# One batch laid out apart from the others: nine consecutive tokens per partition, five loads, softmax in three parts, and a different order of the first weight conversions

## The chip, the cores and the metric

The kernel runs on one core of one Trainium2 chip. The metric is the device time of one execution in microseconds (us); lower is better.

## The reference, cut to what matters

Three stages follow one another, all in float32: an attention over a small memory, a layer with a "tanh-shrink", and a max-out layer. The weights come as float64 (eight bytes each).

```python
# q, k, v: (8, 8, 576, 64) = batch, head, token, dim;  phi: (8, 8, 576, 32)
a = exp(phi - max over tokens);  a = a / (sum over tokens + 1e-9)
k_m, v_m = a^T k, a^T v                       # per batch and head: 32 x 64
attn = softmax(q k_m^T / 8);  x = attn v_m    # per token: 32 weights
x = x as (4608, 512)
h = x w_in;  g = h - tanh(h);  x = g w_out    # w_in 512 x 2048, w_out 2048 x 512
out = max(x w1, x w2, x w3) @ w_out2          # w1..w3 512 x 768, w_out2 768 x 512
```

## The kernel before, in words

**Products.** A float32 product that must be exact enough is done as three matmuls of halves: each operand is split into a rounded high part and a remainder (`mm3`: high by high, high by low, low by high). So every operand of the two big layers goes through a cast on ScalarE (ACT) and a subtraction on VectorE (DVE) or GpSimd (POOL) first. Float64 weights are turned into float32 by `conv` (lines 160 to 180): two ACT operations, three DVE operations, and one POOL operation (W_in) or two POOL operations and one more on ACT (W_out).

**Attention of a batch.** `kv_gen` (line 295) is `phi_gen` and then `kv_mm`: the maximum of phi over the tokens on DVE, transposed on TensorE (PE) and reduced, spread again by a matmul, subtracted, exponentiated on ACT; then k_m, v_m and the sums as PE products into one PSUM bank, normalised (`rc`, `n`), transposed (`ps_t`) into `kT` and `vT`. `q_gen` (line 302) does the softmax in two halves of 288 tokens: the queries are transposed on DVE in 32 x 32 blocks (`qT`), multiplied with `kT` (`sc`), transposed back (`s`), then maximum, subtraction, exponential, sum, reciprocal (`st`), product on POOL, transposition (`aT`), and the split into `at` (cast on ACT, remainder on POOL). v_m is folded into W_in: `vw_gen` (line 353) makes vw = v_m W_in (`ps_w`) for a batch and a quarter `fq` of W_in's 2048 columns, so that h = at vw.

**The two big layers.** A step is one tile of tokens by one block `fc` of 128 hidden columns: `emit_h` 6 matmuls into `ps_h`, `emit_g` the tanh-shrink and split (`th`, `gh`), `emit_x` 12 matmuls into the four banks `ps_x`, which have one buffer each and are copied out (`xo`) at a tile's last step. The hidden columns are done in two phases of eight blocks. In the first phase, batches 0 and 1 come in four tiles of 288 tokens (line 476), each first with blocks 0 to 3 and, after all four tiles, with blocks 4 to 7; that makes 32 steps. All later batches go in pairs, as tiles of 320, 512 and 320 tokens. The max-out layer follows.

**Layout of a batch.** phi, k and v lie with 4 consecutive tokens per partition for the first 512 tokens and a fifth, on 64 partitions, for the last 64 (two DMAs each; the pad of phi is filled by POOL). The queries come in 16 DMAs per batch (`load_q`, line 224), with runs of 32 numbers (128 bytes).

**What sets the order.** All loads are issued by SyncE (SP) in one queue. The instructions of a program are generators that the main code advances; each engine runs its instructions in a fixed order that a planner lays down from its own estimate of the time, going by the program's order among those that it thinks ready. So an instruction can stand in an engine's queue ahead of one that was ready sooner. `V.mark` and `S.mark` with `background` put an operation of DVE or ACT behind a given instruction on its engine (`Paced`, lines 48 to 62, through which nearly every instruction has line 57). During the steps, `slot()` advances three tracks (further batches' attention, conversions, query loads) between matmul groups. The start is written out at the end of the part printed below: loads of batch 0, W_in's first quarter (`w0`, four blocks of 128 rows, three `raw` buffers), the queries between its loads, `phi_gen(0)`, `kv_mm(0)` side by side with `w0`, then W_out's first block (`wo0`), the loads of batch 1, the first half of the softmax, `vw_gen`, the second half beside W_out's conversions.

Of the kernel before, what the change touches and what calls it, by code (L numbers as in the profile page):

```python
# [22 lines left out]
def kernel(  # L23
# [88 lines left out]
    def f(x):  # L112
        return x.bitcast(F32)
# [10 lines left out]
    def bank(i, shape, name):  # L124
        return ps_m.tile(shape, F32, tag=f"m{i}", bufs=1, name=name)
# [8 lines left out]

    live = [0]

    def fetch(src):
        live[0] += 1
        raw = cv_p.tile([P, 512, 2], U32, tag="raw", bufs=3, name="raw")
# [46 lines left out]

    def wi_conv(fq):
        t = wo1.tile([P, HP, FQ], F32, name="wi2") if fq == 2 else wi_p.tile([P, HP, FQ], F32, tag="wi", bufs=2, name="wi")
        yield from convs(*((moe_w_in[r * P:(r + 1) * P, fq * FQ:(fq + 1) * FQ], t[:, r], None) for r in range(HP)), ahead=2 if fq else 3)
        wi[fq] = t  # L190


    phi_t, kv_t, q_t = {}, {}, {}

    def load_phi(b, last=None):
# [34 lines left out]
    def phi_gen(b):  # L230
        load_phi(b)
        ph = phi_t.pop(b)
        yield
        mx = ap.tile([P, H, M], F32, tag="mx", bufs=1, name="mx")
        V.tensor_max(mx, ph[:, :, 0], ph[:, :, 1])
        for c in range(2, C):
            V.tensor_max(mx, mx, ph[:, :, c])
        yield
        pm = bank(1, [P, 2, 2, P], "ps_mx")
        for i in range(2):  # L240
            T.transpose(pm[:, 0, i], mx[:, 4 * i:4 * i + 4].rearrange("p h m -> p (h m)"), ident)
# [12 lines left out]
        yield  # L254
# [5 lines left out]
    def kv_mm(b):  # L260
# [31 lines left out]
            S.copy(t.rearrange("p r m -> p (r m)"), pt[:, i])  # L292
        yield

    def kv_gen(b):
        yield from phi_gen(b)
        yield from kv_mm(b)
# [71 lines left out]
    wo_t = {}  # L369

    def wo_conv(fcs, p):
        ts = [p.tile([P, 2, DM], F32R, name=f"wo{fc}") for fc in fcs]
# [94 lines left out]
    def pieces(t0, n):  # L467
        out, t = [], t0
        while t < t0 + n:
            b, s0 = divmod(t, NS)  # L470
            k = min(t0 + n - t, NS - s0)
            out.append((b, s0, k))
            t += k
        return t0, n, out

    NI = 4
    tiles = [[pieces(i * NH, NH) for i in range(NI)] if ph == 0 else [] for ph in range(2)]
    for ph in range(2):
        for t0 in range(0, B * NS, 2 * NS):
            if ph or t0:  # L480
# [106 lines left out]
    def part_of(g, n):
        for _ in range(n):
            next(g)
            yield  # L590
# [2 lines left out]
        for g in gens:  # L593
            yield from g

    load_phi(0)
    load_kv(0)
    w0 = wi_conv(0)
    next(w0)
    drain(load_q(0, 0))  # L600
    next(w0)
    drain(load_q(0, 1))
    next(w0)
    drain(phi_gen(0))
    drain(kv_mm(0), w0)
    wo0 = wo_conv(range(4), wo_p)
    next(wo0)
    next(wo0)
    load_phi(1, fetch.last)
    load_kv(1, fetch.last)  # L610
    drain(q_gen(0, (0,)))
    drain(vw_gen(0, 0, 0))
    for _ in range(5):
        next(wo0)
    S.mark = at_cast[-1]
    background[0] = True
# [225 lines left out]
    def outs(g):  # L842
        ps = {}

        def part(u, js):
            background[0] = True
            if u not in ps:
                ps[u] = get(f"b{u % 2}")
            o = slice(u * P, (u + 1) * P)
            for j in js:  # L850
                mh = mh_t[j // 2][:, :, j % 2, o]
                mm3(ps[u], (mh[:, 0], mh[:, 1]), (wz[:, j, 0], wz[:, j, 1]), j == 0, j == J - 1)
            background[0] = False
# [74 lines left out]
```

## Time and profile before

| | |
|---|---|
| three runs | 1368.75, 1369.56, 1370.29 us; median 1369.56 us |
| profiled execution | 1365.75 us, of which the traced span is 1364.0 us |
| PE busy | 94% of the span |
| DVE, POOL, ACT busy | 55%, 39%, 37% |
| first `ps_h` matmul | 46.61 us after the span's start |

The profiled execution is one run of its own; its rows add up to its own time, not to the median of the three. Busy time of PE includes pipelining and is not time at its peak. A row of the timeline has the start, the busy time, the engine, the line (L57 for what goes through the helper), the operation with output and input, and in brackets how long the engine had been idle and what released it. PE is a matmul, PEld the load of its weights, SPq the issuing of a DMA.

### The profile page before, as it was taken

How to read it: one execution, taken by the hardware profiler on the slowest of the kernel's cores; microseconds unless marked ns; L12 is line 12 of the kernel's file. 1: busy time of each engine (PE TensorE's matmuls, PEld its weight loads, DVE VectorE, ACT ScalarE, POOL GpSimd, SP SyncE). 2: the span in 40 equal slices, each digit the busy share in tenths (PEclk: the TensorE clock that was granted, in tenths of full speed). 3: DMA queues.
4: the chain of work that ended last, by engine and by line, in shares of the span. 5: the costliest groups of instructions: out<-in, count | busy, mean ns of one | idle time of the engine just before them, and what ended most of it. 6: DMA issues, size and time to landing. Idle time of an engine off the chain costs nothing.

```text
span 1364.0 us, 22739 instructions
## 1 busy us (share of the span) xinstructions
PE 1285.4 (94%) x8996; PEld 1157.4 (85%) x8996; DVE 751.2 (55%) x1189; ACT 507.1 (37%) x993; POOL 531.8 (39%) x470
## 2 busy tenths in 40 slices
PE   3578898999998999999999999999999999999998
PEld 1457696897897799898989999999999899999996
DVE  3868557666545755756643344555734546457342
ACT  2446244454334455555544332223322323233221
POOL 1637334554423546776754341132311312223110
PEclk9989998999999899999999999999999999999999
DMA  8874847866714536667575139838557477385431
GB/s 204 243 194 127 207 139 189 215 213 172 186 57 178 189 105 236 242 206 251 207 254 168 50 125 364 342 126 307 192 171 286 141 270 268 97 307 197 166 132 47
DMA packets 188394, 264.94 MB, mean 194 GB/s; under 512 B 94976, under 2 KB 160512, under 8 KB 179200
## 3 DMA queue, kind: packets, MB, share of 16 engines
q1 hardware_dynamic: 188000, 259.82, 58.3%
q0 software_dynamic: 288, 3.67, 0.7%
q8 instruction: 71, 1.16, 0.4%
q14 instruction: 35, 0.29, 0.1%
HBM read 199.49 MB, written 63.96 MB: 193 GB/s over the span
## 4 chain that ended last, share of the span: by engine, by line
PE 84%; DVE 7%; SPq 3%; issue 2%; POOL 2%; ACT 1%; DMA 1%; POOLq 0%; ACTq 0%; DVEq 0%
PE b L57 40%; PE ps_x L57 26%; PE ps_h L57 13%; PE ps_w L57 2%; PE ps_kv L57 2%; DVE cvb L57 2%; SPq L224 1%; DVE st L57 1%; DVE s L57 1%; POOL s L57 1%; DVE mx L57 1%; DMA raw<-in_moe_w_out_dram 1%; SPq L214 1%; DVE th L57 1%; DVE vw L57 0%
## 5 line engine op out<-in xcount | busy, mean ns | idle before, releaser
L57 PE MATMUL ps_x<-gh,wo 128*128 128x320 f32 (+2 forms) x2400 | 451.9, 335 | 7.2 <-DVE xo L57 5.5
L57 PEld LDWEIGHTS ps_x<-gh,wo 128*128 128x128 f32 x2400 | 381.4, 191 | 54.7 <-issue 22.9
L57 PE MATMUL b<-mv,sw 128*128 128x384 f32 x2268 | 401.6, 338 | 0.0
L57 PEld LDWEIGHTS b<-mv,sw 128*128 128x128 f32 x2268 | 399.1, 188 | 1.4 <-DMA sw<-sw_d 0.3
L57 POOL TENSOR_TENSOR gh<-th,gh 128x320 fp32r<-128x320 f32 (+2 forms) x200 | 209.8, 1051 | 259.0 <-ACT gh L57 248.9
L57 PE MATMUL ps_h<-at,vw 128*128 128x256 f32 (+2 forms) x1536 | 254.9, 307 | 20.4 <-DVE th L57 10.0
L57 PEld LDWEIGHTS ps_h<-at,vw 128*128 128x128 f32 x1536 | 227.7, 197 | 47.7 <-DVE th L57 15.6
L57 DVE TENSOR_TENSOR th<-ps_h,th 128x320 f32<-128x320 f32 (+2 forms) x200 | 106.7, 536 | 184.2 <-ACT th L57 183.5
L57 ACT ACTIVATE th<-ps_h 128x320 f32<-128x320 f32 (+2 forms) x200 | 95.2, 478 | 200.2 <-PE ps_h L57 185.7
L57 PE MATMUL b<-wz,mh 128*128 128x512 f32 x648 | 150.4, 390 | 1.1 <-DVE ob L57 1.1
L57 PEld LDWEIGHTS b<-wz,mh 128*128 128x128 f32 x648 | 121.3, 188 | 26.5 <-DVE ob L57 2.0
L57 ACT CAST gh<-th 128x320 fp32r<-128x320 f32 (+2 forms) x200 | 99.6, 499 | 96.0 <-DVE th L57 83.8
L57 POOL TENSOR_TENSOR c<-c,u 128x384 f32<-128x384 f32 x36 | 36.5, 1015 | 226.6 <-ACT u L57 226.6
L57 ACT COPY p<-b 128x384 f32<-128x384 f32 x108 | 51.8, 479 | 169.6 <-PE b L57 146.4
L57 DVE TENSOR_TENSOR c<-b,u 128x384 f32<-128x384 f32 x72 | 39.9, 554 | 97.0 <-PE b L57 97.0
L57 DVE TENSOR_SCALAR cvb<-cvb 128x512 f32<-128x512 f32 x112 | 69.8, 624 | 29.8 <-ACT cvb L57 27.0
L57 DVE TENSOR_TENSOR m<-c,m 128x768 f32<-128x768 f32 x72 | 69.0, 958 | 5.7 <-DVE c L57 0.9
L57 DVE TENSOR_TENSOR c<-b,p 128x384 f32<-128x384 f32 x72 | 37.7, 554 | 37.7 <-ACT p L57 34.2
L57 DVE TENSOR_TENSOR vw<-ps_w,vw 128x512 fp32r<-128x512 f32 x64 | 41.4, 681 | 22.9 <-ACT vw L57 22.9
L57 POOL TENSOR_TENSOR mv<-xr,mv 128x384 fp32r<-128x384 f32 x30 | 48.9, 1664 | 12.4 <-PE b L57 9.3
L57 POOL TENSOR_TENSOR m<-m,u 128x384 f32<-128x384 f32 x18 | 21.4, 1189 | 81.6 <-ACT u L57 80.2
L57 ACT CAST mh<-m 128x384 fp32r<-128x384 f32 (+1 forms) x54 | 31.8, 620 | 57.1 <-DVE m L57 57.1
(82 smaller groups left out, 1051.5 us busy)
## 6 DMA issues: line engine op xcount, KB each, us to landing
sw<-sw_d SPq DMA_DIRECT2D x52, 1792.0 KB, 7.6
sw_d<-so SPq DMA_DIRECT2D x9, 1792.0 KB, 7.1
raw<-in_moe_w_out_dram SPq DMA_DIRECT2D x22, 512.0 KB, 5.5
qt<-in_q_dram SPq DMA_DIRECT2D x128, 72.0 KB, 3.1
at_d<-at SPq DMA_DIRECT2D x16, 576.0 KB, 3.7
at<-at_d SPq DMA_DIRECT2D x8, 1152.0 KB, 6.3
raw<-in_moe_w_dram SPq DMA_DIRECT2D x18, 512.0 KB, 4.0
out_dram<-ob SPq DMA_DIRECT2D x144, 64.0 KB, 1.7
```

The source lines that it names most:

```text
L57: i = op(*a, **kw)
L214: DMA.dma_start(out=t[:64, i, :, 4], in_=x[b, :, 4 * P:].rearrange("h p d -> p h d"))
L224: q_dma.dma_start(out=t[64 * e + 32 * h:64 * e + 32 * h + 32, r], in_=src[e, h, r])
```

## The change

For batch 0 alone phi, k, v and q are laid out with nine consecutive tokens per partition: the 64 partitions of a half hold the 576 tokens of one head of a pair. phi, k and v take one DMA each, the queries two (`spread`). `kv_first` replaces `kv_gen(0)`: the maximum over a partition's nine tokens is a tree of four operations, the same tree adds up the nine exponentials, and the products run over 64 partitions at a time, the two heads of a pair in two banks. `q_first` replaces `q_gen(0)`: parts of 192 tokens, keys of 32 partitions at a time, the scores in two groups with their back transpositions between them. The first four tiles of steps become five: three of 192 tokens for batch 0, two of 288 for batch 1. W_in's first quarter has all four loads issued at the start (the fourth into a tile that a later W_out block uses); two of its conversions run beside the keys, the other two beside the first part's softmax, on DVE behind the normalisation of the keys. ACT's exponential is called once at the very start. The output's rows of batch 0 are addressed accordingly. Parts left out are marked.

```diff
     def wi_conv(fq):
         t = ...
-        yield from convs(*((moe_w_in[r * P:(r + 1) * P, fq * FQ:(fq + 1) * FQ], t[:, r], None) for r in range(HP)), ahead=2 if fq else 3)
+        jobs = [(moe_w_in[r * P:(r + 1) * P, fq * FQ:(fq + 1) * FQ], t[:, r], None) for r in range(HP)]
+        if fq == 0:
+            raws = []
+            for r in range(HP):
+                raws.append(fetch(jobs[r][0], wo_p.tile([P, 512, 2], U32, tag="wo7", bufs=1, name="raw") if r == 3 else None))
+                yield
+            for x, (_, hi, lo) in zip(raws, jobs):
+                yield
+                yield from conv(x, hi, lo)
+        else:
+            yield from convs(*jobs)
+    C9 = NS // 64
+    J0 = C9 // 3
+    W0 = 64 * J0
+    def spread(t, x):
+        DMA.dma_start(out=t.rearrange("p r j d -> p r (j d)"),
+                      in_=x.rearrange("(r e) n d -> r (e n) d", e=2).rearrange("r (p j) d -> p r (j d)", p=P))
...
+    def tree(op, pc, name):
+        t = ...
+        op(t, pc[:, 0:4], pc[:, 4:8])
+        op(t[:, 0:2], t[:, 0:2], t[:, 2:4])
+        op(t[:, 0], t[:, 0], t[:, 1])
+        op(t[:, 0], t[:, 0], pc[:, 8])
+        return t[:, 0].rearrange("p r m -> p (r m)")
+    def kv_first():
...
+        mx = tree(V.tensor_max, pc, "mx")
+        yield
+        pm = bank(1, [P, 2, P], "ps_mx")
+        T.transpose(pm[:, 0], mx, ident)
+        mt = ap.tile([P, 2], F32, tag="mt", bufs=1, name="mt")
+        V.tensor_reduce(mt, pm[:, 0].rearrange("p (e c) -> p e c", e=2), axis=AX.X, op=ALU.max)
+        yield
+        dg = ap.tile([P, 2, P], F32, tag="mx", bufs=1, name="dg")[:, 0]
+        V.tensor_copy(dg.rearrange("p (e c) -> p e c", e=2), mt[:, :, None].to_broadcast([P, 2, 64]))
+        T.matmul(pm[:, 1], dg, ident, start=True, stop=True)
+        yield
+        freed[1] = V.tensor_tensor(out=ph, in0=ph, in1=pm[:, 1]..., op=ALU.subtract).ins
+        yield
+        S.activation(ph, ph, AF.Exp)
+        yield
+        part = tree(V.tensor_add, pc, "part")
+        ps = [bank(e, [P, 2 * D + 1], "ps_kv") for e in range(2)]
...
+        for c in range(C9):
+            for r in range(HP):
+                for e in range(2):
+                    ins.append(T.matmul(ps[e][32 * r:32 * r + 32, :2 * D], ph[64 * e:64 * e + 64, r, c], t[64 * e:64 * e + 64, :, r, c], start=c == 0, stop=c == C9 - 1, skip_group_check=True).ins)
...
+        for e in range(2):
+            T.matmul(ps[e][:, 2 * D:], part[64 * e:64 * e + 64], ones[64 * e:64 * e + 64, :1], start=True, stop=True, skip_group_check=True)
...
+        V.reciprocal(rc, rc)
+        for e in range(2):
+            freed[e] = V.tensor_tensor(out=n[:, :, e], in0=ps[e][:, :2 * D]..., in1=rc[:, e:e + 1, None]..., op=ALU.mult).ins
...
+    def q_first(h):
...
+        for g in range(2):
+            t = ap.tile([P, 2, NH], F32, tag="qT", bufs=2, name="qT")[:, :, :W0]
+            V.transpose(out=t, in_=q_t[0, g].rearrange("p r j d -> p r (j d)")[:, :, o])
...
+        for u in range(2):
+            w = [32 * (2 * e + u) for e in range(2)]
+            ins = [T.matmul(scs[e][32 * r:32 * r + 32, u]..., kT[0][w[e]:w[e] + 32, t, r],
+                            qT[r // 2][w[e]:w[e] + 32, r % 2, t], start=t == 0, stop=t == 1, skip_group_check=True).ins
+                   for t in range(2) for r in range(HP) for e in range(2)]
+            tc.add_manual_dep(ins[0], freed[1].name, ..., reason="both banks")
...
+            for e in range(2):
+                freed[e] = V.transpose(out=se[:, e, u], in_=scs[e][:, u]).ins
+            yield
...
+        softmax.append(V.tensor_tensor(out=s, in0=s, in1=st[:, :, 0:1]..., op=ALU.subtract).ins)
+        yield
+        softmax.append(S.activation(s, s, AF.Exp, scale=0.125).ins)
...
+        if h == 2:
+            for g in range(2):
+                ld.add(("q", 1, g), load_q(1, g))
+        yield
-    NI = 4
-    tiles = [[pieces(i * NH, NH) for i in range(NI)] if ph == 0 else [] for ph in range(2)]
+    NI = 5
+    tiles = [[pieces(i * W0, W0) for i in range(3)] + [pieces(NS + i * NH, NH) for i in range(2)], []]
     G.memset(ones, 1.0)
+    S.activation(ap.tile([P, 2], F32, tag="mt", bufs=1, name="warm"), ones[:, :2], AF.Exp)
-    load_phi(0)
-    load_kv(0)
+    load_first()
     w0 = wi_conv(0)
     next(w0)
-    drain(load_q(0, 0))
+    load_q0(0)
     next(w0)
-    drain(load_q(0, 1))
+    load_q0(1)
     next(w0)
-    drain(phi_gen(0))
-    drain(kv_mm(0), w0)
+    next(w0)
+    next(w0)
+    drain(kv_first(), part_of(w0, 10))
     wo0 = wo_conv(range(4), wo_p)
     next(wo0)
     next(wo0)
     load_phi(1, fetch.last)
     load_kv(1, fetch.last)
-    drain(q_gen(0, (0,)))
+    q0 = q_first(0)
+    next(q0)
+    next(q0)
+    V.mark = freed[1]
+    background[0] = True
+    drain(q0, w0)
+    background[0] = False
     drain(vw_gen(0, 0, 0))
+    V.mark, S.mark = softmax[:2]
+    background[0] = True
     for _ in range(5):
         next(wo0)
     S.mark = at_cast[-1]
     background[0] = True
-    drain(q_gen(0, (1,)), part_of(wo0, 6))
+    drain(chain(q_first(1), q_first(2)), part_of(wo0, 6))
     background[0] = False
```

## Rows read from the trace of the kernel before

**Rows 1.** The page: busy time of each engine, share of the span, instructions.
```profile
PE 1285.4 (94%) x8996; PEld 1157.4 (85%) x8996; DVE 751.2 (55%) x1189; ACT 507.1 (37%) x993; POOL 531.8 (39%) x470
```

**Rows 2.** Busy time by stretch; last columns: granted clock, DMA share, GB/s.
```profile
core 0: us, PE busy (x) PEld busy (x) DVE busy (x) ACT busy (x) POOL busy (x), PEclk, DMA share, GB/s
0.00:46.60 46.60, 14.47 (x220) 7.15 (x220) 22.50 (x42) 12.09 (x20) 10.64 (x15) 1.00 0.91 236
46.60:84.00 37.40, 31.80 (x326) 27.80 (x327) 30.24 (x47) 19.41 (x41) 24.48 (x21) 0.95 0.70 190
84.00:130.00 46.00, 31.50 (x228) 24.08 (x227) 38.22 (x60) 20.89 (x47) 26.91 (x23) 0.89 0.63 162
130.00:200.00 70.00, 64.24 (x742) 56.46 (x741) 37.90 (x80) 25.15 (x55) 23.68 (x26) 0.95 0.59 160
300.00:800.00 500.00, 490.65 (x3577) 431.86 (x3577) 273.47 (x456) 232.24 (x461) 259.12 (x231) 0.99 0.53 177
```

**Rows 3.** Timeline from 0 to 48 us: batch 0's keys and first half of softmax.
```profile
4.92 0.43 DVE L57 TENSOR_TENSOR mx<-phi 128x256 f32<-128x256 f32 x1 [3.91 <-DMA phi<-in_phi_dram]
5.38 1.41 DVE L57 TENSOR_TENSOR mx<-mx,phi 128x256 f32<-128x256 f32 x3
...
11.46 1.28 ACT L57 ACT_TABLE_LOAD   x1 [11.46 <-DVE phi L57]
12.75 1.27 ACT L57 ACTIVATE phi<-phi 128x1280 f32<-128x1280 f32 x1
...
15.31 2.52 PE L57 MATMUL ps_kv<-kv,phi 128*32 128x128 f32 x40 [0.41 <-DMA kv<-in_v_dram]
...
27.75 0.15 DVE L57 TENSOR_SCALAR rc<-ps_kv 128x2 f32<-128x2 f32 x1
...
30.45 1.12 PE L57 MATMUL ps_t<-ident,n 128*64 128x128 f32 x8 [9.43 <-DVE n L57]
...
32.09 1.76 PE L57 MATMUL sc<-qT,kT 64*32 64x288 f32 x16 [0.52 <-ACT vT L57]
...
37.05 0.83 DVE L57 STREAM_TRANSPOSE s<-sc 128x288 f32<-128x288 f32 x2
...
38.03 1.96 PE L57 MATMUL ps_w<-wi,vT 64*32 64x512 f32 x16 [4.18 <-DVE s L57]
...
45.88 0.67 ACT L57 CAST at<-aT 128x576 fp32r<-128x576 f32 x1 [2.36 <-DVE aT L57]
...
46.61 0.85 PE L57 MATMUL ps_h<-at,vw 128*128 128x288 f32 x2 [0.98 <-ACT at L57]
```

**Rows 4.** The same timeline: SyncE's queue with the queries, and W_in's last block.
```profile
10.18 10.15 SPq L224 DMA_DIRECT2D qt<-in_q_dram  x8
...
21.51 6.96 SPq L224 DMA_DIRECT2D qt<-in_q_dram  x8
...
33.13 0.66 ACT L57 ACTIVATE cvb<-raw 128x512 f32<-128x512 f32 x1 [1.09 <-DMA raw<-in_moe_w_in_dram]
```

**Rows 5.** Busy time by stretch (columns as in rows 2): how fast the loads come.
```profile
2.00:20.35 18.35, 7.75 (x156) 5.32 (x156) 5.59 (x10) 3.79 (x4) 0.35 (x1) 1.00 0.90 214
4.00:8.00 4.00, 0.66 (x2) 0.29 (x2) 2.07 (x5) 0.00 (x0) 0.00 (x0) 1.00 0.97 276
40.00:44.00 4.00, 0.00 (x0) 0.00 (x0) 2.92 (x7) 2.27 (x4) 2.99 (x3) 1.00 1.11 349
```

**Rows 6.** Groups of matmuls by shape: count, busy us, mean ns of one, idle before.
```profile
L57 PE MATMUL ps_x<-gh,wo 128*128 128x512 f32 x672 | 166.8, 394 | 0.0
...
L57 PE MATMUL ps_h<-at,vw 128*128 128x256 f32 x672 | 97.9, 293 | 5.6 <-ACT vw L57 2.6 <-DVE th L57 2.4 <-DVE vw L57 0.5
L57 PE MATMUL ps_x<-gh,wo 128*128 128x288 f32 x384 | 62.4, 312 | 7.2 <-DVE xo L57 5.5 <-POOL gh L57 1.6
```

**Rows 7.** Timeline: the fifth step's tanh (second tile), and batch 1's first matmul.
```profile
68.48 0.41 ACT L57 ACTIVATE th<-ps_h 128x288 f32<-128x288 f32 x1 [5.42 <-PE ps_h L57]
...
95.67 0.85 PE L57 MATMUL ps_h<-at,vw 128*128 128x288 f32 x2 [5.60 <-ACT at L57]
```

More of the change, by code (lines that the diff above doesn't have):

```diff
@@ L135, with fetch @@
     live = [0]
-    def fetch(src):
+    def fetch(src, room=None):
         live[0] += 1
-        raw = cv_p.tile([P, 512, 2], U32, tag="raw", bufs=3, name="raw")
+        raw = room or cv_p.tile([P, 512, 2], U32, tag="raw", bufs=3, name="raw")
         u = src.bitcast(U32)
@@ L293, in kv_mm @@
         yield
+    def tree(op, pc, name):
+        t = ap.tile([P, 2, NH], F32, tag="aT", bufs=1, name=name).rearrange("p e c -> p (e c)")[:, :4 * HP * M].rearrange("p (j r m) -> p j r m", j=4, m=M)
+        op(t, pc[:, 0:4], pc[:, 4:8])
[4 more added lines that the diff above has]
+    def kv_first():
+        ph = phi_t.pop(0)
+        pc = ph.rearrange("p r j m -> p j r m")
+        mx = tree(V.tensor_max, pc, "mx")
[9 more added lines that the diff above has]
+        yield
+        freed[1] = V.tensor_tensor(out=ph, in0=ph, in1=pm[:, 1].rearrange("p (r m) -> p r m", m=M)[:, :, None, :].to_broadcast([P, HP, C9, M]), op=ALU.subtract).ins
+        yield
[3 more added lines that the diff above has]
+        ps = [bank(e, [P, 2 * D + 1], "ps_kv") for e in range(2)]
+        t = kv_t.pop(0)
+        ins = []
+        for c in range(C9):
+            for r in range(HP):
+                for e in range(2):
+                    ins.append(T.matmul(ps[e][32 * r:32 * r + 32, :2 * D], ph[64 * e:64 * e + 64, r, c], t[64 * e:64 * e + 64, :, r, c], start=c == 0, stop=c == C9 - 1, skip_group_check=True).ins)
+            if c == 0:
+                tc.add_manual_dep(ins[0], freed[1].name, mybir.DependencyInfo(mybir.DependencyClass.Sync, mybir.DependencyReason.DATA), reason="both banks")
+            if c % 2:
+                yield
+        for e in range(2):
+            T.matmul(ps[e][:, 2 * D:], part[64 * e:64 * e + 64], ones[64 * e:64 * e + 64, :1], start=True, stop=True, skip_group_check=True)
+        yield
+        rc = ap.tile([P, 2], F32, tag="rc", bufs=2, name="rc")
+        n = ap.tile([P, 2, 2, D], F32, tag="kvn", bufs=2, name="n")
+        for e in range(2):
+            V.tensor_scalar(rc[:, e:e + 1], ps[e][:, 2 * D:], 1e-9, None, ALU.add)
+        V.reciprocal(rc, rc)
+        for e in range(2):
+            freed[e] = V.tensor_tensor(out=n[:, :, e], in0=ps[e][:, :2 * D].rearrange("p (i d) -> p i d", i=2),
+                                       in1=rc[:, e:e + 1, None].to_broadcast([P, 2, D]), op=ALU.mult).ins
+        yield
+        pt = bank(0, [P, 3, P], "ps_t")
+        for t in range(2):
+            for e in range(2):
+                for u in range(2):
+                    w = 32 * (2 * e + u)
+                    T.matmul(pt[w:w + 32, t], n[:, 0, e, 32 * t:32 * t + 32], ident, start=True, stop=True)
+        for e in range(2):
+            T.matmul(pt[64 * e:64 * e + 64, 2], n[:, 1, e], ident, start=True, stop=True)
+        kT[0] = ap.tile([P, 2, HP, M], F32, tag="kvn", bufs=2, name="kT0")
+        S.copy(kT[0].rearrange("p t r m -> p (t r m)"), pt[:, :2].rearrange("p t c -> p (t c)"))
+        S.copy(vT[0].rearrange("p r m -> p (r m)"), pt[:, 2])
+        yield
@@ L348, in q_gen @@
             yield
+    softmax = []
+    def q_first(h):
+        if h == 0:
+            at_t[0, 0] = at_p.tile([P, 2, 2, NS], F32R, tag="at", bufs=3, name="at")
+            at_d[0] = dram.tile([P, 2, 2, NS], F32, name="at_d0")
+        at = at_t[0, 0]
+        o = slice(h * W0, (h + 1) * W0)
+        qT = []
+        for g in range(2):
+            t = ap.tile([P, 2, NH], F32, tag="qT", bufs=2, name="qT")[:, :, :W0]
+            V.transpose(out=t, in_=q_t[0, g].rearrange("p r j d -> p r (j d)")[:, :, o])
+            qT.append(t.rearrange("p r (j t c) -> p r t j c", t=2, c=32))
+            yield
+        J4 = 4 * J0
+        s = ap.tile([P, 2 * JH, M], F32, tag="s", bufs=1, name="s")[:, :J4]
+        se = s.rearrange("p (e u j) m -> p e u (j m)", e=2, u=2)
+        scs = [bank(e, [P, 2, W0 // 2], "sc") for e in range(2)]
+        for u in range(2):
+            w = [32 * (2 * e + u) for e in range(2)]
+            ins = [T.matmul(scs[e][32 * r:32 * r + 32, u].rearrange("p (j c) -> p j c", c=32), kT[0][w[e]:w[e] + 32, t, r],
+                            qT[r // 2][w[e]:w[e] + 32, r % 2, t], start=t == 0, stop=t == 1, skip_group_check=True).ins
+                   for t in range(2) for r in range(HP) for e in range(2)]
+            tc.add_manual_dep(ins[0], freed[1].name, mybir.DependencyInfo(mybir.DependencyClass.Sync, mybir.DependencyReason.DATA), reason="both banks")
+            for a, b in zip(ins, ins[1:]):
+                tc.add_manual_dep(b, a.name, mybir.DependencyInfo(mybir.DependencyClass.NoSync, mybir.DependencyReason.DATA), reason="side by side")
+            yield
+            for e in range(2):
+                freed[e] = V.transpose(out=se[:, e, u], in_=scs[e][:, u]).ins
+            yield
+        st = ap.tile([P, 2 * JH, 3], F32, tag="st", bufs=1, name="st")[:, :J4]
+        V.reduce_max(st[:, :, 0], s, axis=AX.X)
+        softmax.append(V.tensor_tensor(out=s, in0=s, in1=st[:, :, 0:1].to_broadcast([P, J4, M]), op=ALU.subtract).ins)
+        yield
+        softmax.append(S.activation(s, s, AF.Exp, scale=0.125).ins)
+        yield
+        V.reduce_sum(st[:, :, 1], s, axis=AX.X)
+        V.tensor_scalar(st[:, :, 2], st[:, :, 1], 1e-9, None, ALU.add)
+        V.reciprocal(st[:, :, 2], st[:, :, 2])
+        yield
+        G.tensor_tensor(out=s, in0=s, in1=st[:, :, 2:3].to_broadcast([P, J4, M]), op=ALU.mult)
+        yield
+        aT = ap.tile([P, 2, NH], F32, tag="aT", bufs=1, name="aT")[:, :, :W0]
+        V.transpose(out=aT, in_=s.rearrange("p (e j) m -> p e (j m)", e=2))
+        yield
+        at_cast.append(S.copy(at[:, 0, :, o], aT).ins)
+        G.tensor_sub(at[:, 1, :, o], aT, f(at[:, 0, :, o]))
+        yield
+        DMA.dma_start(out=at_d[0][:, :, :, o], in_=f(at[:, :, :, o]))
+        if h == 2:
+            for g in range(2):
+                ld.add(("q", 1, g), load_q(1, g))
+        yield
@@ L371, in wo_conv @@
     def wo_conv(fcs, p):
-        ts = [p.tile([P, 2, DM], F32R, name=f"wo{fc}") for fc in fcs]
+        ts = [p.tile([P, 2, DM], F32R, tag=f"wo{fc}", bufs=1, name=f"wo{fc}") for fc in fcs]
         for k, _ in enumerate(convs(*((moe_w_out[fc * P:(fc + 1) * P, :], t[:, 0], t[:, 1]) for fc, t in zip(fcs, ts)))):
@@ L859, in done @@
                 b, j = divmod((g * NG + u * P + r) // 32, TJ)
-                dst = out[b * NS:(b + 1) * NS, :].rearrange("(p j) e -> j p e", j=TJ)
-                DMA.dma_start(out=dst[j], in_=ob[r:r + 32, :])
+                rows = out[b * NS:(b + 1) * NS, :]
+                if b:
+                    dst = rows.rearrange("(p j) e -> j p e", j=TJ)[j]
+                else:
+                    h, j = divmod(j, 2 * J0)
+                    k, j = divmod(j, J0)
+                    dst = rows.rearrange("(u p j) e -> u j p e", u=2, j=C9)[k, h * J0 + j]
+                DMA.dma_start(out=dst, in_=ob[r:r + 32, :])
         prep = iter(())
```

11 lines of the change are left out of this document (added).

## The prediction

> **What bounds the kernel now.** I read the page first: PE is busy for 94% of the span [rows 1], so outside a few stretches only less PE work can help. Then the busy time by stretch, to find where PE is not full [rows 2]: from 300 to 800 us it is busy for 490.65 of 500; in the first 46.60 us for 14.47, and the engines that feed it are not full either (DVE 22.50). From there to 84 us PE is idle for 5.6 us, to 130 us for 14.5 (while DVE is busy for 38.22 of 46), to 200 us for 5.8. So the start costs some 46 us before the first step, and 20 us more in which the steps outrun what is made for them. Last the timeline of the start, to see what ends each wait [rows 3, 4].
>
> Batch 0's phi is there at 4.9 us, the exponential waits for a table load of 1.28 us and ends at 14.02, the k and v products begin at 15.31 when v has landed. Then a gap: they are over before 22 us, but the normalisation `rc` comes at 27.75, on DVE behind W_in's conversions, whose blocks land between the query loads. Keys' transposition 30.45, scores 32.09, their back transposition 37.05, the split `at` done at 46.55, the first `ps_h` at 46.61. SP spends 10.15 and 6.96 us issuing the 16 query loads [rows 4]; W_in's last block, behind them in that queue, starts its conversion at 33.13.
>
> **The loads (removes 16 query DMAs, three small ones and a fill; adds two query DMAs).** SP is passed by five DMAs and four blocks of W_in. Bytes: phi 0.59 MB, k and v 1.18 each, each block 0.52, each half of the queries 0.59; cumulated in the order of the queue, v is complete at 2.95 MB, the second half of the queries at 5.18, W_in's last block at 6.23. Rates [rows 5]: 214 GB/s over the present start, 276 while only runs of phi, k and v move, 349 at the best. No load keeps the 128-byte runs, so I take 276, with the first bytes at 2 us: v at 12.7, queries at 20.8, W_in at 24.6. By the ends: v 10.5 to 15.8, queries 16.8 to 26.2, W_in 19.9 to 31.1.
>
> **The keys.** The maximum has the same 1,024 elements per partition as the 0.43 + 1.41 us now [rows 3]. The transposition, the reduction and the spreading have half their columns, the subtraction and exponential nine tenths; with the table load gone ahead I put the exponential's end at 11 us instead of 14. Then v binds: 12.7. The products are 72 matmuls over 64 partitions in place of 40 over 128, of two instructions each as now (40 instructions in 2.52 us for one head of each pair, 63 ns each). If the two heads run wholly beside each other, 144 instructions cost 4.5 us, if not at all 9.1; the scores, which are already laid out so, took 1.76 us for 16 instructions of 288 columns, 0.38 ns per column against 0.49 here, which would make 7.0. I take 5.5: 18.2. The tree over the sums, 1.8 us on DVE, lies beside them. `rc` and `n`, about 1.1 us; ten products for the four that take 1.12 now, 1.5; copies 0.4: keys at 21.2 instead of 32. The queries with their transposition (0.5) come at 21.3, about together.
>
> **The first part.** Scores: 64 instructions of 96 columns at the 110 ns of the row would be 7.0 us, scaled by columns 2.3; nearer columns, since the instructions run beside each other. With the two pairs of back transpositions, which now stand between the groups (the second group waits for the first pair, and in PE's queue what comes behind waits with it), 3.5 us: 24.8. From the back transposition to the end of `at` 288 tokens took 9.5 us (37.05 to 46.55), DVE's other work included. For 192 tokens, between two thirds (6.3) and all of it; I take 7.6: 32.4. The other branch: from W_in's last landing to `ps_w` 4.9 us (33.13 to 38.03), `ps_w` 1.96, evacuation some 2.5 us: 24.6 + 9.4 = 34.0. So the first `ps_h` starts at 34.2 instead of 46.61: **−12.4 us**. Bounds: 30 with 349 GB/s, 42 with 214 and the dear ends.
>
> **The steps.** Batch 0 has 24 steps of 18 matmuls at 192 columns for 16 at 288: 432 against 288 matmuls. By the groups [rows 6], busy time over count is 248 ns for 512 columns, 162 for 288, 146 for 256. The slope from 512 to 256 carries on to 120 at 192; the other end is that 192 cost as much as 256. No row has fewer columns with full weights. I take 125, near the slope, as 288 lies on it. Half of these steps come in the first round, where PE stands idle more than that; the other half (blocks 4 to 7) later, where PE is nearly full: 216 × 125 − 144 × 162 = **+3.7 us** (ends +2.6 and +8.2). The Trainium skill, page "TensorE: Matmul & The Clock Gate", section "LDWEIGHTS (loading the stationary operand)", speaks against the change: a weight load takes by its columns, whatever they multiply, an estimated 107 ns for 128, which would be longer than 192 columns at 2.4 GHz (80 ns). By that the later half would cost an estimated 216 × 107 − 144 × 120 = 5.8 us where I have 3.7, and the sum would be about 1362.6; no row here has a case narrow enough to show it.
>
> Two more changes of tile: now PE waits 5.5 us in all for `xo` copies of the first four tiles [rows 6]; two more rounds of ten instead of eight, +0.6 (0 to 2). DVE has the tree, four short back transpositions per part and 24 steps' subtractions instead of 16, some 4 us more by their rows' sizes; it is covered where DVE idles, and not between 84 and 130 us [rows 2]: +1.0 (0 to 4). POOL's third product and split, ACT's third exponential: covered, POOL is at 26.91 of 46 there; without the cover about 1 us, inside that bound. SP's third store, batch 1's 16 query loads after the third part: no row shows them waited for; nothing. Output rows: same sizes, nothing.
>
> **Batch 1.** Its first matmul comes at 95.67, 49 us after the first of all, behind a chain that DVE may start only after the fourth and fifth steps' subtraction; the fifth step, of the second tile, has its tanh at 68.48 [rows 7]. With a part ready sooner that mark comes sooner, and eight steps instead of four cover the chain. At most the 14.5 us of idle time, at least nothing; DVE is nearly full there, so I take **−2.0**.
>
> **Sum.** −12.4 + 3.7 + 0.6 + 1.0 − 2.0 = −9.1 us. The profiled execution's own time is 1365.75 (span 1364.0), 3.8 below the median 1369.56: 1356.7 for a profile like it, **1360.5** against the median.
>
> **Rivals.** (a) *Narrow tiles bind* (the other side). If 192 columns cost 146 ns and no idle time hides it, all of batch 0 costs 432 × 146 − 288 × 162 = +16.4, less 12.4, with the smaller terms +1.6: +5.6, 1375. It decides from about 133 ns, where 432 × x − 46.7 + 1.6 = 12.4. For it: the weight loads are as many as the matmuls, and the page's rule above has this form; against: idle time in the first round [rows 2], and 288 columns on the slope. 0.13. (b) *The start is bound by DVE's order still.* "Behind the keys" holds only for W_in's third and fourth blocks; the first two may be put ahead of `n`, as `rc` is now put behind. The second lands at (4.59 MB) 18.6, its conversion takes some 2.5 us, so `n` ends at 22 and the keys come at 24, and W_in's other blocks queue behind: the first step some 3 us later, 1363.5. For it: rows 3's gap before `rc`. 0.19. (c) *Batch 1 is released early*: the term of 2.0 is 8, not 2: 1354.5. For it the idle time from 84 to 130; against it DVE's load there. 0.17. (d) *The gain is handed back*: conversions, loads and batch 1's chain are paced by DVE and DMA, and PE waits longer before batch 1 or the second round: only 2 to 3 us of the 12.4 are left, minus 2 to 5 of the dearer steps, within 2 us of before: 1370. For it: DVE busy for 38.22 of 46; against: DVE's own work also starts earlier, and only 22.50 of its first 46.6 us are used. 0.11. The forecast: 0.40.
>
> **How the numbers follow.** The median of this kernel moves by about 0.2% from no change, 2.7 us. Forecast, (b) and (c) are faster, (d) mostly within, (a) slower, with a little of (d): faster 0.76, same 0.09, slower 0.15. The start at 30 us, the steps at their low end and (c) together would give 1347, little of it likely, so the low end is 1350; the high end takes in (d) and leaves most of (a) out: 1371.
>
> **What would show it.** In the profile after: no table load behind the subtraction; SP done with its nine loads well before 20 us; v's products at 12 to 13 us and 4 to 5 us long; `n` within 2 us of their end (else b); scores at about 21; the first `ps_h` at 34 (30 to 42); batch 0's `ps_x` at 192 columns near 125 ns of busy time each; batch 1's first `ps_h` at 80 to 84 instead of 95.67; the stretch from 130 us on as dense as now. The prediction is wrong if 192 columns cost as much as 256, or if batch 1's first matmul or the second round stays where it was although the first step came sooner.

## The result: the first step comes 15 us sooner, the whole is slower

The changed kernel takes 1377.08 us (median of six runs, 1376.37 to 1381.47) against 1369.51 us for the kernel before beside it: ratio 1.0057, 95% interval 1.0038 to 1.0076. The forecast was 1360.5 us. The profiled execution took 1381.47 us (span 1379.7), 4.4 above its median, while that of before lay 3.8 below its own: the two profiles differ by 15.7 us where the medians differ by 7.6.

The page of the changed kernel, busy time of the engines (as [rows 1]):
```profile
PE 1300.6 (94%) x9299; PEld 1176.2 (85%) x9299; DVE 747.3 (54%) x1225; ACT 511.4 (37%) x1014; POOL 531.2 (39%) x479
```
Its busy time by stretch (as [rows 2]):
```profile
0.00:46.60 46.60, 24.26 (x393) 18.59 (x394) 33.30 (x72) 19.97 (x38) 20.75 (x24) 0.69 0.89 281
46.60:84.00 37.40, 31.45 (x400) 27.06 (x399) 28.32 (x56) 17.42 (x42) 19.18 (x21) 0.88 0.68 179
84.00:130.00 46.00, 28.83 (x209) 24.53 (x209) 21.73 (x43) 17.76 (x40) 20.41 (x21) 0.74 0.52 127
130.00:200.00 70.00, 61.72 (x633) 55.42 (x632) 38.76 (x87) 24.49 (x58) 20.71 (x26) 0.93 0.56 145
300.00:800.00 500.00, 490.65 (x3710) 431.96 (x3709) 276.16 (x462) 234.06 (x466) 259.19 (x230) 0.98 0.54 179
```
The first row is fuller, as meant. In the third, PE does less than before (28.83 for 31.50 us) and DVE far less (21.73 for 38.22): no engine is near full there. From 300 to 800 us PE is as busy as before (490.65 us).

The timeline of the changed kernel: its start, then batch 1's softmax (as [rows 3, 7]):
```profile
0.76 1.28 ACT L57 ACT_TABLE_LOAD   x1 [0.76 <-PEq L1075]
...
11.44 3.61 PE L57 MATMUL ps_kv<-kv,phi 64*32 64x128 f32 x144 [2.64 <-ACT phi L57]
...
18.24 0.21 DVE L57 TENSOR_SCALAR rc<-ps_kv 128x1 f32<-128x1 f32 x2
...
21.97 0.90 PE L57 MATMUL sc<-qT,kT 32*32 32x96 f32 x32 [1.05 <-ACT vT L57]
...
31.12 0.74 PE L57 MATMUL ps_h<-at,vw 128*128 128x192 f32 x2 [3.53 <-ACT at L57]
...
58.31 0.78 DVE L57 STREAM_TRANSPOSE qT<-qt 128x576 f32<-128x576 f32 x1 [3.93 <-DMA qt<-in_q_dram]
...
82.61 2.81 SPq L141 DMA_DIRECT2D raw<-in_moe_w_out_dram  x3
83.26 0.72 PE L57 MATMUL sc<-qT,kT 64*32 64x288 f32 x16 [0.36 <-DVE vw L57]
...
87.23 0.74 DVE L57 TENSOR_REDUCE st<-s 128x18 f32<-128x576 f32 x1
...
90.86 0.66 ACT L57 ACTIVATE cvb<-raw 128x512 f32<-128x512 f32 x1 [3.16 <-DMA raw<-in_moe_w_out_dram]
91.63 0.43 DVE L57 TENSOR_SCALAR cvb<-cvb 128x512 f32<-128x512 f32 x1 [3.65 <-ACT cvb L57]
91.97 0.75 DVE L57 TENSOR_TENSOR s<-s,st 128x576 f32<-128x576 f32 x1
...
98.16 1.27 POOL L57 TENSOR_TENSOR wo<-cva,wo 128x512 fp32r<-128x512 f32 x1
...
99.38 1.18 POOL L57 TENSOR_TENSOR s<-s,st 128x576 f32<-128x576 f32 x1
...
100.59 0.78 DVE L57 STREAM_TRANSPOSE aT<-s 128x576 f32<-128x576 f32 x1 [3.40 <-POOL s L57]
...
102.13 0.85 PE L57 MATMUL ps_h<-at,vw 128*128 128x288 f32 x2 [13.64 <-ACT at L57]
```
The first `ps_h` starts at 31.12 instead of 46.61, but batch 1's first one at 102.13 instead of 95.67. Between its scores (`sc`) and it lie 18.9 us; before they were 9.3 (to 95.67, [rows 7]), from this line of the timeline of before:
```profile
86.42 0.72 PE L57 MATMUL sc<-qT,kT 64*32 64x288 f32 x16 [1.40 <-DVE vw L57]
```
In the changed kernel a conversion of W_out (`cvb`) stands in DVE's queue between two operations of batch 1's softmax (`st` at 87.23, `s` at 91.97) and waits for one of the three blocks that SP issued from 82.61 on, after batch 2's loads. Later the softmax's product on POOL (`s`, 99.38) starts behind two conversion operations (96.94 and 98.16), though its input is ready at 97.2.

The lost time by milestones of the two profiles, in SP's queue: the second round's first reload of partial sums (`xo<-xd`) at 135.2 us for 135.0 before, so all 15.5 us were gone by then; its last store at 199.5 for 190.8 (+8.5); the next pair's first two tiles stored at 285.0 for 271.7 (+4.6); 384.7 for 369.7 (+1.7); the end +0.7. Of the +4.6, 3.2 are one wait of `ps_w` for batch 3's softmax (5.4 for 2.2 us).

### The profile page after: what moved, and what is told of

It reads as the page before. It is cut to its first block, busy times and chain, and to the rows that moved or that the text cites. A ratio compares the mean times of both kernels' runs of the same rounds, so it can differ in the third digit from the quotient of the medians.

```text
span 1379.7 us, 23400 instructions
## 1 busy us (share of the span) xinstructions
PE 1300.6 (94%) x9299; PEld 1176.2 (85%) x9299; DVE 747.3 (54%) x1225; ACT 511.4 (37%) x1014; POOL 531.2 (39%) x479
## 4 chain that ended last, share of the span: by engine, by line
PE 82%; DVE 6%; DMA 4%; SPq 2%; issue 2%; ACT 2%; POOL 1%; POOLq 0%; DVEq 0%; ACTq 0%
PE b L57 40%; PE ps_x L57 25%; PE ps_h L57 13%; DMA raw<-in_moe_w_out_dram 2%; PE ps_kv L57 2%; PE ps_w L57 2%; DVE cvb L57 2%; SPq L255 1%; DVE st L57 1%; DMA raw<-in_moe_w_in_dram 1%; DVE s L57 1%; DVE vw L57 1%; DMA qt<-in_q_dram 1%; POOL s L57 1%; DVE th L57 1%
## 5 line engine op out<-in xcount | busy, mean ns | idle before, releaser
L57 PE MATMUL ps_x<-gh,wo 128*128 128x320 f32 (+3 forms) x2496 | 464.9, 334 | 9.3 <-DVE xo L57 7.1
L57 PEld LDWEIGHTS ps_x<-gh,wo 128*128 128x128 f32 x2496 | 393.8, 193 | 58.3 <-issue 26.8
L57 POOL TENSOR_TENSOR gh<-th,gh 128x320 fp32r<-128x320 f32 (+3 forms) x208 | 208.8, 1006 | 274.4 <-ACT gh L57 267.2
L57 PE MATMUL ps_h<-at,vw 128*128 128x256 f32 (+3 forms) x1584 | 260.4, 306 | 31.6 <-ACT at L57 17.2
L57 PEld LDWEIGHTS ps_h<-at,vw 128*128 128x128 f32 x1584 | 234.3, 199 | 59.5 <-ACT at L57 19.9
L57 DVE TENSOR_TENSOR th<-ps_h,th 128x320 f32<-128x320 f32 (+3 forms) x208 | 108.3, 523 | 202.3 <-ACT th L57 201.5
L57 ACT ACTIVATE th<-ps_h 128x320 f32<-128x320 f32 (+3 forms) x208 | 96.5, 466 | 198.7 <-PE ps_h L57 191.9
L57 ACT CAST gh<-th 128x320 fp32r<-128x320 f32 (+3 forms) x208 | 101.4, 488 | 97.3 <-DVE th L57 88.2
L57 DVE TENSOR_SCALAR cvb<-cvb 128x512 f32<-128x512 f32 (+1 forms) x112 | 67.1, 601 | 28.7 <-ACT cvb L57 26.7
```

Of the source, the lines that this page charges most:

```text
L57: i = op(*a, **kw)
```

## Experiments

Times are compared with runs of the kernel before on the same chip. The numbers follow the names of the kernels (there is no eighth). The rounds: blocks 0 to 3 of batches 0 and 1 are the first, blocks 4 to 7 the second.

**1. The old tiles in the new kernel**
```diff
-    NI = 5
-    tiles = [[pieces(i * W0, W0) for i in range(3)] + [pieces(NS + i * NH, NH) for i in range(2)], []]
+    NI = 4
+    tiles = [[pieces(i * NH, NH) for i in range(NI)] if ph == 0 else [] for ph in range(2)]
```


> The changed kernel, but with four tiles of 288 tokens for the steps again; the softmax stays in parts of 192. Theory Q (the early start is lost because DVE's queue stands behind late loads: batch 1's queries at 54 to 58 us, W_out blocks at 87 to 92): those waits stay, the first step now needs two parts of the softmax and starts near 50 us instead of 31, and the time stays within 3 us of the changed kernel's 1377, or is longer. Theory N (the loss is the narrow steps: 432 matmuls at about 110 ns instead of 288 at about 134): some 5 us come back in the second round of batch 0 and up to 4 in the first: 1368 to 1372, with the second round 4 to 6 us shorter.

1364.39 us, ratio 0.9961 (0.9946 to 0.9977): faster than both kernels, and by more than either theory allowed. The tiles alone cost 12.7 us; the rest of the change is worth some 5 to 6. Yet its first step comes later than before (48.02 us, as two parts must be ready). Batch 1 in its timeline:
```profile
79.22 0.72 PE L57 MATMUL sc<-qT,kT 64*32 64x288 f32 x16 [2.05 <-DVE vw L57]
...
88.51 0.85 PE L57 MATMUL ps_h<-at,vw 128*128 128x288 f32 x2 [5.13 <-ACT at L57]
```
From scores to `ps_h` it is 9.3 us again, and the second round is 56.5 us long (64.3 in the changed kernel).

**2. The new tiles in the old kernel** (the reverse of that edit, the softmax still in halves)

> The kernel before with one thing of the change: batch 0's steps in three tiles of 192 tokens instead of two of 288; its loads, keys and softmax in halves stay. Theory N: slower by 5 to 9 us, 1374 to 1379, nearly the whole distance to the changed kernel. Theory Q: slower by the second round's 4 to 5 us alone, at most 1375, and batch 1's first matmul stays near 96 us.

1385.46 us, ratio 1.0107 (1.0092 to 1.0121), slower than either theory allowed. The old start with narrow tiles shows the same stretch of batch 1. Timeline:
```profile
87.60 0.71 PE L57 MATMUL sc<-qT,kT 64*32 64x288 f32 x16
...
105.91 1.96 PE L57 MATMUL ps_w<-wi,vT 64*32 64x512 f32 x16 [11.91 <-DVE s L57]
107.80 2.39 PE L57 MATMUL ps_h<-at,vw 128*128 128x288 f32 x11
```
So 20.2 us from scores to `ps_h`, with none of the new start: the tiles bring it.

**3. Batch 1's queries loaded early** (batch 0's queries in another buffer, so that batch 1's follow its k and v)
```diff
+        load_q0.t = at_p.tile([P, 2, 2, NS], F32, tag="at", bufs=3, name="q0")
...
-            for g in range(2):
-                ld.add(("q", 1, g), load_q(1, g))
...
+    for g in range(2):
+        drain(load_q(1, g))
```


> The changed kernel with batch 0's queries in a buffer of their own (an attention buffer not yet in use), so that batch 1's queries are loaded right behind its k and v and not after batch 0's third part. Theory Q: the 3.9 us in which DVE waits for them at 54 us go, the third part and batch 1's keys come 4 us or more earlier, and the time falls by 3 to 8 us, to 1369 to 1374. Theory N: no change beyond 1.5 us, as PE's steps cost the same.

1394.35 us, ratio 1.017 (1.015 to 1.0191), the worst of all. Timeline:
```profile
26.58 15.23 SPq L257 DMA_DIRECT2D qt<-in_q_dram  x16
41.93 1.02 SPq L141 DMA_DIRECT2D raw<-in_moe_w_out_dram  x2
...
46.69 0.66 ACT L57 ACTIVATE cvb<-raw 128x512 f32<-128x512 f32 x1 [13.71 <-DMA raw<-in_moe_w_out_dram]
...
49.06 1.60 PE L57 MATMUL ps_h<-at,vw 128*128 128x192 f32 x6 [12.84 <-DVE th L57]
```
DVE's wait for queries is gone, but SP takes 15.23 us to issue them and W_out's next blocks wait behind. It removes one wait and makes a larger one, so it can't say what the first was worth.

**4. Batch 2's phi, k and v behind two more blocks of W_out**
```diff
-        if b:
+        if b == 1:
+            def later():
+                load_phi(2, fetch.last)
+                load_kv(2, fetch.last)
+                yield
+            ld.add(("kv", 2), later(), 10)
+        elif b:
             load_phi(b + 1)
             load_kv(b + 1)
...
```


> The changed kernel with the large loads of batch 2 (phi, k, v) put behind two more W_out blocks in SP's queue. Theory Q: the W_out blocks land some 5 us or more earlier, DVE's 3.7 us wait at 88 us goes, batch 1's first matmul comes at 95 to 98 us instead of 102, and the time falls by 3 to 6 us, to 1371 to 1374. Theory N: no change beyond 1.5 us.

1376.13 us, ratio 1.004 (1.0028 to 1.0053); batch 1's first `ps_h` 100.24. That is 1 us less than the changed kernel, within the noise (the intervals overlap), as theory N said: the loads ahead of W_out's blocks are not what costs the time. Whether it is that the conversions stand in that place at all, the next run tests.

**5. W_out's blocks 4 to 7 from step 12 instead of step 6**
```diff
-    bg.add("wo", wo_conv(range(4, FC), wo_p), 6)
+    bg.add("wo", wo_conv(range(4, FC), wo_p), 12)
```


> The changed kernel, but the conversions of W_out's blocks 4 to 7 may begin only at step 12 instead of step 6 (one number). With narrow tiles there are 12 steps and 60 slots before batch 1 instead of 8 and 40, so by step 6 only as much time has gone as in 4 old steps. Theory D (order): the conversions planned into the middle of batch 1's softmax, which wait for their loads, hold DVE and GpSimd there; from batch 1's score matmuls (sc) to its first ps_h it is 18.9 us in the changed kernel, 9.3 us in the kernel before. By D that stretch falls to 9 to 11 us, batch 1's first ps_h goes from 102.1 to 90 to 94 us, and the time to 1366 to 1371. Theory N (narrow matmuls alone cost it): DVE's order is no matter, the PE is short in any case, first ps_h may move but the time stays at 1375 to 1379. A third way: the delayed blocks are late for the second round (fc 4 to 7 are wanted from step 20), and the gain goes there.

1367.52 us, ratio 0.9987 (0.9972 to 1.0001): 9.6 us less than the changed kernel by one number. Timeline:
```profile
80.77 0.71 PE L57 MATMUL sc<-qT,kT 64*32 64x288 f32 x16
...
89.10 0.78 DVE L57 STREAM_TRANSPOSE aT<-s 128x576 f32<-128x576 f32 x1 [1.70 <-POOL s L57]
...
90.64 0.85 PE L57 MATMUL ps_h<-at,vw 128*128 128x288 f32 x2 [6.21 <-ACT at L57]
```
9.9 us instead of 18.9, and the scores come 2.5 us sooner (80.77 for 83.26). All three forecasts of theory D came true: three tiles of four steps before batch 1 instead of two give the tracks 60 slots instead of 40, and the gate, counted in steps, opened too early in time. The second round stays at 63.1 us (126.3 to 189.4).

**6. The second round in tiles of 288, the first narrow; 9. The reverse**
```diff
+            wide = [pieces(i * NH, NH) for i in range(4)]
-            rounds = [(t, fr) for fr in (range(4), range(4, FC)) for t in tiles[0][:NI]] + rounds[NI:]
+            rounds = [(t, range(4)) for t in tiles[0][:NI]] + [(t, range(4, FC)) for t in wide] + rounds[NI:]
```


> The changed kernel with its narrow tiles in the first round only (fc 0 to 3 in 192+192+192+288+288 columns); the second round (fc 4 to 7) goes in four tiles of 288 as before. Theory N: the second round (first reload of the partial sums to its last store) falls from 64.3 us to 55 to 57 us, and the time by 7 to 9 us to 1368 to 1370. Theory D (order in batch 1's softmax) leaves the first round as it is: batch 1's first ps_h stays at 101 to 103 us, and what the second round gives back is only the matmuls' own rise, 110 ns against two thirds of 134 ns, 144 x 3 matmuls at 110 less 144 x 2 at 134 = 8.9 us of PE time, if the PE binds there. My prediction's own term for the same steps was 3.7 us: by that the time is 1373.

> The reverse of the second: the first round in four tiles of 288, the second round in 192+192+192+288+288. It prices the second round's narrow steps alone, with batch 1's softmax undisturbed as with four tiles of 288 (1364.4 us, second round 56.5 us). My prediction's term (+3.7 for matmuls at 125 ns, +0.6 for tile changes) gives 1368.7. Theory N with 110 ns against 134 ns in the PE and the tile changes gives 1372 to 1374, second round 64 to 66 us. If the time were 1365 to 1366, the second round's narrow steps would be covered by other waits, and nearly all of the loss would lie in the first round.

The sixth: 1370.90 us, ratio 1.0017 (1.0003 to 1.0031), second round 57.3 us, batch 1's first `ps_h` unmoved at 100.66. The ninth: 1371.27 us, ratio 1.0014 (1.0000 to 1.0028), second round 65.7 us. So the second round's narrow steps cost 6 to 7 us in all (1377.1 less 1370.9, 1371.3 less 1364.4). Both times lie between my term's (1373 and 1368.7) and theory N's (1368 to 1370 and 1372 to 1374). And theory N's 8.9 us has a slip: it takes 432 matmuls, those of both rounds, where the second round has 216 (144 of `ps_x` and 72 of `ps_h` with 192 columns in the ninth); by its own 110 and 134 ns that is 4.5 us, next to my term of 3.7 + 0.6. Busy time over the second round of the ninth, then of the first:
```profile
126.50:192.20 65.70, 57.42 (x591) 51.05 (x591) 35.03 (x78) 21.12 (x49) 18.95 (x24) 0.92 0.56 145
```
```profile
127.80:184.30 56.50, 49.70 (x510) 43.47 (x510) 31.24 (x66) 19.21 (x43) 17.66 (x21) 0.91 0.65 168
```
PE is busy for 7.7 of the 9.2 us more; 2.0 of them are matmuls of the next tiles (320 columns) that fall into the longer stretch. Of PE's waits one is longer, that at the reload of the partial sums, 5.8 us in the first experiment, 7.1 in the ninth and in the changed kernel, here from the groups of waits of the changed kernel from 135.2 to 199.5 us (in all, times, longest):
```profile
PE ps_x L57 <- DVE xo L57: 7.1, 1, 7.1
```

**7. Both: narrow first round, wide second, step 12**

> Both of the other two together: the first round narrow, the second in 288 columns, W_out's blocks 4 to 7 from step 12. If D and N each hold their own part and add, the time is 1358 to 1364, batch 1's first ps_h at 90 to 94 us and the second round 55 to 57 us; this is the early start kept and both its prices taken away, so it should equal or beat the version with four tiles of 288 (1364.4). If the early start (first ps_h at 31 instead of 47 us) is worth nothing because batch 1's keys and softmax set the pace of the first round, it gives 1364 to 1367, no better than the wide tiles.

1365.25 us, ratio 0.9959 (0.9941 to 0.9977); batch 1's first `ps_h` 91.80. The two parts do not add: 9.6 us (fifth) and 6.2 (sixth) alone, 11.8 together. With both prices gone it equals the first experiment, whose first step is 17 us later, as the second forecast said. The early step itself is worth nothing that can be measured here.

**10. Batch 1's query transposes behind its keys on DVE** (added to the seventh); **11. Tiles of 192, 384, 288, 288**
```diff
+                if b == 1 and hf == 0:
+                    behind(d.ins, ph_sub[b])
```


> The version with both prices taken away (first round narrow, second in 288 columns, W_out's blocks 4 to 7 from step 12), and in addition batch 1's first query transposes ordered behind the subtraction of its keys on DVE. In that version DVE still stands 2 to 4 us at those transposes around 54 us, because the queries land later than the order assumes, and batch 1's first ps_h came at 91.8 us although the first step began at 31.2. Theory Q2 (this wait paces batch 1's keys): its first ps_h moves to 88 to 89 us and the time falls by 2 to 4 us from 1365.25 to 1361 to 1363. Theory E (batch 1 is paced by the elementwise work and loads in front of it as a whole, so the early first step buys nothing): DVE's wait vanishes, another takes its place, batch 1's first ps_h stays at 90 to 92 us and the time at 1364 to 1367.

> The new start with the first round in tiles of 192, 384, 288 and 288 columns and the second in four of 288. It keeps the early first step (ps_h at 31 us) with 16 steps a round, as many slots before batch 1 as with four tiles of 288 (1364.4 us, first step at 48.0, batch 1's first ps_h at 88.5). If the early step itself is worth its time and only the number of steps was the trouble, batch 1's first ps_h comes at 78 to 84 us and the time is 1354 to 1360. If batch 1 is paced by the elementwise work in front of it (theory E), its first ps_h stays at 86 to 90 us and the time at 1362 to 1366, however early the first step is. The 384-column step costs the PE some 1.7 us over the round (72 matmuls at an estimated 178 ns and 72 at 112 against 144 at 133).

The tenth: 1362.59 us, ratio 0.9947 (0.9930 to 0.9965), the lowest median of the study, though its interval overlaps the first's. Timeline:
```profile
57.46 1.47 DVE L57 TENSOR_TENSOR phi<-phi,ps_mx 128x1280 f32<-128x1280 f32 x1
58.85 1.43 DVE L57 STREAM_TRANSPOSE qT<-qt 128x576 f32<-128x576 f32 x2
...
74.43 4.49 PE L57 MATMUL ps_x<-gh,wo 128*128 128x192 f32 x38
78.85 0.72 PE L57 MATMUL sc<-qT,kT 64*32 64x288 f32 x16
...
88.37 0.85 PE L57 MATMUL ps_h<-at,vw 128*128 128x288 f32 x2 [5.86 <-ACT at L57]
```
Batch 1's keys are subtracted 5.5 us sooner than in the seventh (62.95), and 3.4 of that reach `ps_h`, as theory Q2 said; that the time falls with it (2.7 us) is not clear of the noise, as the seventh's interval overlaps too. The eleventh: 1365.89 us, ratio 0.9966 (0.9948 to 0.9985); first step at 31.20, batch 1's first `ps_h` at 89.67: both as theory E said, the early step brings batch 1 no sooner.

**12. Batch 1's preparation advanced 4 instead of 2.5 times a slot** (added to the tenth)
```diff
+        rate[0] = 16 if now[0] < 12 else 10 if now[0] < start[0, 2] else 6
```


> The last version but one (first round narrow, second in 288 columns, W_out's blocks 4 to 7 from step 12, query transposes behind the keys: 1362.6 us, batch 1's first ps_h at 88.4), and in addition the foreground track, which prepares batch 1, is advanced 4 instead of 2.5 times a slot in the first 12 steps. There the keys' subtraction was already 7 us earlier (57.5 us), but batch 1's sc still stood on the PE behind 38 matmuls of the third tile and began at 78.9. Theory O (the order written for the engines, not their capacity, holds batch 1 back, and the early start could be kept): sc begins at 70 to 75, batch 1's first ps_h at 80 to 85, the time falls by 2 to 6 us to 1357 to 1361. Theory E (the elementwise work and loads in front of batch 1 pace it): W_out's conversions now come later and the third tile's steps wait for them; batch 1's first ps_h at 86 to 90, the time 1361 to 1366.

1368.47 us, ratio 0.9993 (0.9980 to 1.0007): worse than the tenth by 5.9. Timeline:
```profile
60.78 0.67 ACT L57 ACTIVATE cvb<-raw 128x512 f32<-128x512 f32 x1 [2.45 <-DMA raw<-in_moe_w_in_dram]
...
82.51 0.71 PE L57 MATMUL sc<-qT,kT 64*32 64x288 f32 x16
...
92.17 0.85 PE L57 MATMUL ps_h<-at,vw 128*128 128x288 f32 x2 [5.44 <-ACT at L57]
```
The forecasts of theory O failed, but the run can't refute it, as it did not bring batch 1 forward: the same track holds W_in's next conversions, one of which now stands in front of batch 1's own exponential on ACT and waits for its load. The scores come later than in the tenth, at 82.51.

## Why the prediction was wrong

- **The start** was right, and better than said: 31.12 us for 34.2 (bounds 30 to 42), −15.5 for −12.4. The table load is at 0.76, v's products begin at 11.44 (12.7) and take 3.61 us for 144 (5.5), the scores start at 21.97 (21.3). Some of that is luck: the loads came at some 400 GB/s, faster than the text's best case (349), the products took less than its low end (4.5), and what they waited for last was the exponential, not v. Rival (b) was half there: `rc` stands 3 us behind the products, after conversions of W_in, but the quicker products had made that up.
- **Batch 1, the step that failed.** The text took −2.0, its first matmul at 80 to 84 us, since "that mark comes sooner, and eight steps instead of four cover the chain". It came at 102.13. The fifth step's tanh did come sooner (52.51 us for 68.48), the subtraction of batch 1's keys hardly (65.66 for 67.22): the early step was not what paced the chain. The runs give the parts: 11.5 us for W_out's conversions before and in its softmax (fifth; 9.0 of them after the scores), 3.4 for the queries that DVE waits for ahead of its keys (tenth); what is left, 88 us, is where it stands with an early or a late first step (first, tenth, eleventh). I counted the extra steps as cover. They are also slots, and each slot moves the conversions on, whose operations then stand in queues that run in order. I weighed DVE's idle time but not what stands in its queue and what that waits for. With this the largest term falls too: −12.4 was taken over whole into the sum, as if a first step 15 us sooner moved the end. With the early step the time is 1365.25 and 1365.89 us (seventh, eleventh), without it 1364.39 (first): it is worth nothing of its own, because batch 1's chain comes no sooner.
- **The narrow steps of the second round**: right in kind, somewhat mis-sized. The term was +3.7 (2.6 to 8.2); the runs show 6 to 7 us with all that follows. In the text's own measure, busy time over count, 192 columns take 136 ns in the ninth's second round, not 125, and 288 take 166 in the first's: 216 × 136 − 144 × 166 = +5.5 us. The sign set for `ps_x`, near 125 ns, was missed: 151 over the changed kernel's whole run. Timeline of the changed kernel in that round, then of the first experiment:
```profile
131.90 1.50 PE L57 MATMUL ps_x<-gh,wo 128*128 128x192 f32 x12
133.24 0.83 PE L57 MATMUL ps_h<-at,vw 128*128 128x192 f32 x6
```
```profile
173.53 2.96 PE L57 MATMUL ps_x<-gh,wo 128*128 128x288 f32 x21
176.33 0.38 PE L57 MATMUL ps_mx<-ident,mx 128*128 128x128 f32 x2
```
  Twelve of 192 columns take 1.34 us from start to start, 112 ns each; 21 of 288 take 2.80, 133 each (granted clock 1.00 in both places): 216 × 112 − 144 × 133 = +5.0 us. By columns alone 192 would be 89. The slope of [rows 6] that I followed did not carry on to 192 columns. That the weight loads set this floor is not shown by a run. The rule of the Trainium skill, page "TensorE: Matmul & The Clock Gate", section "LDWEIGHTS (loading the stationary operand)", an estimated 107 ns for 128 columns of weights, agrees with these 112 ns, and the estimate of +5.8 was the nearer one, though the 120 ns that went with it for 288 columns came out at 133.
- **The tile changes** (+0.6): PE's waits for `xo` grew from 5.5 to 7.1 us, within the bounds. The 7.1 are one wait, at a reload of partial sums that SP issues at 170.52, behind eleven query loads that take it 10.54 us; so SP's queue makes it, not the copies. The 3.2 us longer wait for batch 3's softmax was in no term, and its cause was not tried.
- **DVE** (+1.0): its order bound, its busy time did not; from 84 to 130 us it is busy for 21.73 of 46.
- **The rivals.** (a), 1375, is near the time, and the 136 ns are above the 133 from which it decides. But by its own sum 136 ns give 1371 us, and its condition, that no idle time hides the steps, does not hold: with narrow steps in both rounds and only the gate moved (fifth) the time is 1367.52, 3.1 us above the wide tiles. The larger price, 9.6 us, lies in an order. (d) named the right place and kept 2 to 3 us of the gain; all of it went, and more. The failing conditions of the text came true: batch 1's first matmul later and the second round where it was, though the first step came sooner.

What stays open: what holds batch 1's first matmul at 88 us is argued (theory E), not shown; which part of the new start makes the first experiment's batch 1 come 7 us sooner than before (88.51 for 95.67) was not tried by itself; nor was a wait for queries removed in the unchanged new kernel.

## What to carry to other kernels

A gate or a rate counted in steps changes its meaning when the steps get shorter: look up what the planner now puts into the in-order queues between two operations of a critical chain, and when that lands. An earlier first step is worth only what the next stage's own chain lets through; follow the next batch's first matmul, not the first of all. Price a narrower tile by a time from start to start at full clock in that shape, not by a slope through wider shapes: there may be a floor.

## What was not expected of the hardware

Busy time by stretch (as [rows 2]) of the changed kernel, 31 to 48 us:
```profile
31.00:48.00 17.00, 14.57 (x149) 13.09 (x149) 14.42 (x28) 8.93 (x20) 13.39 (x13) 0.50 0.70 183
```
of the first experiment, of the ninth, and of the twelfth:
```profile
31.00:48.00 17.00, 3.91 (x128) 2.35 (x128) 12.22 (x24) 6.98 (x12) 11.76 (x11) 1.00 0.81 201
31.00:48.00 17.00, 3.25 (x104) 1.94 (x112) 12.51 (x24) 7.26 (x13) 11.40 (x11) 0.50 0.80 196
31.00:48.00 17.00, 13.79 (x145) 12.31 (x146) 12.96 (x25) 8.82 (x20) 12.60 (x12) 1.00 0.68 182
```
The first steps of the changed kernel ran at a granted clock of 0.50 (1.2 of 2.4 GHz). It fell between 17 and 18 us, when PE had been busy for 3.37 us between 12 and 16 and for nothing since; in the first experiment, with the same start, it stayed at 1.00. How much PE has to do from 31 to 48 us does not decide it either: the first and the ninth have the same first round and little PE work there, at 1.00 and 0.50; the changed kernel and the twelfth have much, at 0.50 and 1.00. What decides it, no run here shows. What it costs in this round can be read from the first and the ninth: first `ps_h` at 48.02 and 48.68 us, batch 1's at 88.51 and 88.85, less than 1 us. In the twelfth, whose early steps ran at 1.00, batch 1 came no sooner (92.17) than in the seventh at 0.67 (91.80), though their orders differ. So nothing here says that the lower clock took the gain of the early step.

And the nine loads with long runs together moved some 400 GB/s (400, 397 and 403 in the three stretches of 4 us from 4 to 16 us), above the best row of before, 349 [rows 5].
